# A hand-written order of 1116 tasks, written out anew: a gated long convolution and two MLPs on one Trainium2 core

## The chip, the core and the metric

The kernel runs on one core of one Trainium2 chip. Its work is done by five engines, each with an instruction queue of its own: TensorE (PE, matmuls and transposes through the array; its weight loads are listed as PEld), VectorE (DVE), ScalarE (ACT), GpSimd (POOL) and SyncE (SP), which here only issues transfers. The metric is the time of one execution on the device in microseconds. Of the kernel before there are three runs: 317.10, 317.48 and 317.87 us, median 317.48.

## What is computed

One block of a sequence model with 2048 tokens of width 640 in bfloat16, cut to what matters:

```python
mod = (silu(c) @ w_mod).reshape(c.shape[0], 6, 1, -1)      # sa, ca, ga, sb, cb, gb
h = layernorm(x) * (1 + ca) + sa
x = x + ga * A(h, k, v)                                    # gated long convolution
h = layernorm(x) * (1 + cb) + sb
x = x + gb * B(h)                                          # two MLPs

# A: k_shift = 4-tap causal filter of k;  kv = k_shift * v
#    y = irfft(rfft(kv, 4096) * rfft(ssm_k, 4096))[:2048] + kv * ssm_D;  return q * y
# B: h = gelu(layernorm(x) @ w1);  x1 = x + shifted_by_column_group(h) @ w2
#    return x1 + gelu(layernorm(x1) @ w3) @ w4             # w3: 640 x 1728, w4: 1728 x 640
```

The filter ssm_k has one row of 2048 taps for each of the 640 channels; ssm_D is added to tap 0 of each row, so that the transform of the filter carries that term too.

## The kernel before, in words

**Stages.** The transforms are made as matmuls in two steps of 64 x 64, with tables of sines and cosines that the kernel computes itself. Channels are cut into five blocks of 128 (b = 0 to 4).

- *Tables.* GpSimd writes integer ramps (iota), VectorE masks them to a period (L321, L322), ScalarE takes the sine (L353). For one half of the largest table, Gs, the angles come from ScalarE by an Identity with a scale and an offset (L324, offset offc from L269); the other half comes from three steps on GpSimd or VectorE (L338, L340, L342). L382 makes a negated copy, and three transfers (L389 twice, L390 once) copy parts of the table to other partitions. F1 is a small table (F1c, spread out by L364 and L365); the tables E are scaled by eight small instructions at L406; silu(c) is a chain of seven on GpSimd (L416 to L422).
- *Filter.* Five transfers bring ssm_k (L229, tile Ra), one brings ssm_D (L227). ssm_D is turned into columns by a small matmul (L293) and copied out by ScalarE (L296, Dcol); the same is done with c and the 4-tap filter (L302, L304; copied at L306, csk). L481 adds Dcol to column 0 of a block, and L430 transposes the block in 32 x 32 squares on VectorE into Rb.
- *Stage 1* multiplies the transposed blocks with F1 (L443), 20 PSUM groups for the filter and 20 for kv; *stage 2* multiplies with Gs (L463), 22 groups for each. Every group is copied out of PSUM by ScalarE (L211) or VectorE (L213).
- *kv.* k and v come in eight token pairs each (transfers L495, transposes on TensorE L503, copies L510 or L512). The 4-tap filter is a matmul with diagonal weights (L524), and VectorE multiplies it with v (L529).
- *Modulation.* Twelve half products of silu(c) with w_mod (transfer L549, matmul L555, copies L566 or L570).
- *Inverse.* The two spectra are multiplied on VectorE (L678) after a swap of halves by transfers (L674); the first inverse step is L689 and L690, the second (inverse2) L722 in six pieces.
- *MLPs.* For each token tile: gate and residual (L798, L801), layernorm sums (L790, a square with accumulation on ScalarE), norm (L653 or L655), transposes (called turns: L829, copied by L835 on ScalarE or L837 on VectorE), w1 (L875 and L885, gelu L877 and L891), w2 (L930, residual on VectorE L937), norm and turns again, w3 (L967, L971, gelu L980), w4 (L997, L1006, then VectorE L1029, L1034, L1035 and four output transfers a tile on SP, L1038). The last tile has a path of its own (L1043 to L1056).

**What sets the order.** The function builds a list of 1116 tasks by calls of `add`; a task's number is its place in that list. A string ORDER then names all tasks once, each as a word `<number><engine>`, the engine as P, A, D, G or S, and behind a colon the PSUM slot or slots (0 to 3) for the tiles that the task opens:

```python
for word in ORDER.split():
    head, _, places = word.partition(":")
    t = self.tasks[int(head[:-1])]
    t.on = self.CODE[head[-1]]
```

The tasks are issued in that order, and each engine runs its own in the order of the words; waits between engines follow from what the tasks read and write. So ORDER decides three things: where a task stands in its engine's queue, which engine does a task that may run on several, and which of the four PSUM slots a group uses. PSUM has one pool with one buffer for each slot, so a group in slot 2 waits until the group that had slot 2 before has been copied out. Costs that `add` is given are not used by this.

**Names.** Tasks 0 and 1 to 5 are the loads of ssm_D and of the five blocks of ssm_k, 6 and 7 those of the 4-tap filter and of c; 9 is the iota for the partition index, 10 the small steps on VectorE that make the offsets (L262 to L270), 12 and 13 the selects that make identities (L282, L286). Task 14 (L294) is a sine of one column that nobody reads; it makes ScalarE load the sine table. 15 and 16 are L293 and L296; 17 and 18 are L302 to L304 and L306. 19 to 24 are the table F1 and 25 to 32 the first half of Gs, with 33, 34 and 35 its three transfers; 36 to 48 are the second half, with 46, 47 and 48 its transfers. 66 to 75 are, for each block, L481 and L430. 229 to 232 are loads of x. 446 to 463 are the last six modulation products, three tasks each. 480, 511, 515, 518, 521 and 524 are the pieces of inverse2. 548, 569 and 589 are turns (L829) of the first three tiles; 553, 574 and 594 are their matmuls with w1 (L875, gelu 554, 575 and 595), 555, 576 and 596 the ones beside them (L885, gelu 556, 577 and 597).

Of the kernel before, what the change touches and what calls it, by code (L numbers as in the profile page):

```python
# [26 lines left out]
2S 8D 9G 25G 10D 0S 12G 36G 4S 26A 19G 13G 20D 6S 11G 7S 21D 23A 28A 3S 27D 5S 29D 15P:0 16A 1S 30A 68D 37G 69D 116S 22A 31A 72G 17P:0 24G 32A 18A 73D  # L27
90P:0 34G 50G 70G 86P:1 56G 91A 74G 57G 71D 122S 87A 104P:2 102P:0 66G 105A 38G 88P:1 75D 119S 103A 92P:2 89A 39G 106P:0 67D 93A 125S 117P:1 49G 128S
107A 112P:2 123P:3 113A 118D 82P:0 137S 124D 40A 114P:1 131S 76P:2 83A 115D 41G 120P:3 77A 78P:0 42G 134S 121D 98P:1 33S 79A 100P:2 99D 126P:3 101A
96P:0 58G 150S 127D 129P:1 97A 230S 84P:2 130D 110P:3 85A 80P:0 65G 43D 138P:1 44A 140P:2 139D 111A 59D 45A 51D 132P:3 81A 46S 52D 135P:1 47S 133A  # L30
142P:0 35S 136D 153S 60A 141D 159S 54A 94P:1 53A 61G 108P:3 55D 146P:2 62G 109A 143D 95A 221P:3 147D 48S 63G 199P:1 222A 162S 201P:0 156S 203P:2 200A
202D 209P:3 232S 64A 229S 185P:1 210D 204A 144P:0 186D 205P:2 145D 223P:1 206A 225P:3 224A 219P:2 226D 151P:0 220A 189P:1 152D 165S 154P:3 190A 215P:2
155D 168S 191P:0 216A 207P:1 148P:3 208D 192A 227P:1 149D 197P:0 228A 157P:2 198A 213P:1 158D 171S 187P:3 214A 231S 195P:0 188D 160P:2 244S 196A
211P:1 161D 193P:3 212A 163P:0 194D 217P:2 164A 169P:1 218D 366S 367G 166P:3 170A 172P:0 167D 174P:2 247S 173A 236D 250S 239A 176P:0 175D 235A 184D
182P:2 234A 177D 286P:3 178P:1 287A 183D 238A 278D 288P:3 284P:2 180P:0 289A 179D 285A 294P:3 181D 290P:1 295A 292P:2 291A 281D 245P:3 296P:0 293A
248P:1 246A 279D 282P:2 256S 297A 251P:3 253S 283A 316P:0 259S 252D 249A 314P:2 280D 317A 298P:1 300P:3 315A 320P:0 301A 321D 308P:2 309A 318P:3 299D
306P:0 382S 383G 257P:2 307A 233D 275S 273G 319A 342P:0 258D 271G 276S 332P:1 343D 237G 324P:2 270S 333A 326P:3 325D 274S 340P:0 327A 277S 328P:1 341D
272S 338P:2 329A 254P:3 465D 339A 310P:0 255D 267S 264G 322P:1 265G 311A 266S 312P:3 323D 262G 260P:2 269S 263G 313A 268S 334P:0 240G 261D 302P:1 374S
474D 335A 304P:3 471D 330P:2 303D 305A 336P:0 337A 331D 375G 344P:1 360P:3 390S 391G 345A 362P:0 369D 356P:2 363A 346P:1 368D 398S 399G 357A 354P:0
361A 376D 364P:2 347A 372P:3 365D 449S 355A 475D 358P:1 377D 370P:2 373A 348P:0 385D 371A 406S 407G 378P:3 349A 384D 380P:2 414S 415G 359A 352P:0 392D  # L40
353A 388P:1 472D 379A 393D 386P:0 381A 350P:3 401D 422S 423G 351A 394P:2 400D 430S 431G 389A 396P:3 466D 395A 404P:1 408D 387A 402P:2 409D 397A 450P:0
417D 438S 403A 439G 412P:3 446S 241A 451D 410P:2 452S 416D 14A 411A 425D 418P:0 413A 420P:2 424D 405A 432D 458S 428P:3 419A 455S 426P:1 433D 421A 441D
427A 436P:0 464G 429A 434P:2 476D 440D 437A 447P:1 468D 444P:3 435A 448D 242D 442P:1 445A 473D 453P:2 243G 443A 469D 456P:3 477D 470D 480P:10 478D
457A 467D 454A 479D 518P:23 481A 482D 520A 514G 537D 524P:01 558D 519A 538D 483G 559D 539A 489S 484S 540D 459P:2 560A 578D 541G 498S 561D 550A 579D
461S 460A 493S 562G 542D 525A 511P:23 488S 581D 580A 543D 485S 512A 486S 563D 582G 544A 491S 515P:20 545D 513A 564D 546G 526A 583D 494S 565A 566D 497S
609D 567G 606D 517A 584D 492S 516A 547D 487S 586D 548P:0 585A 490G 610D 462P:2 549A 607D 611A 587G 555P:0 551D 612D 608A 568D 463A 588D 569P:1 613G
556A 589P:2 570D 590D 521P:13 571D 618D 552D 553P:2 530S 619D 614A 529S 620D 594P:0 554A 528S 615D 621A 533S 616D 576P:2 527S 595A 572D 617A 531S
596P:0 622D 496S 597A 669D 623G 523D 535S 534S 577A 574P:0 573D 536S 672D 624A 627D 670D 628P:2 495S 575A 625P:3 673D 629A 598P:0 671A 626D 675G 674A
532S 638P:3 599D 636P:2 639A 676G 601D 500D 600A 677D 681D 637A 602G 682D 683D 522A 643P:2 603D 684A 678D 604P:1 679D 640P:3 605A 644D 680A 685G
656P:1 641D 645A 686G 646D 642A 658P:3 690D 657A 647G 687D 660P:2 659A 499D 691P:1 661A 688P:0 692A 654P:3 501G 651D 689A 648D 591A 652P:1 701P:0 653D  # L50
502A 649P:2 592D 699P:1 593D 650D 505D 702A 717P:2 630D 506D 633A 655A 631D 507G 700A 632D 723P:3 742D 508A 743D 706P:1 739D 740D 718A 703P:0 745D
741A 707D 662P:2 744A 704D 708A 746G 709D 724A 634D 705A 635D 503A 751D 710G 752D 721P:3 663D 711A 504G 753D 747A 714D 766D 712P:2 754A 715P:0 713D
719P:1 722A 748D 749D 716A 664D 750A 789P:0 509A 755D 666S 693D 665S 756G 694D 668S 809D 667S 720A 793P:3 810D 790A 791P:1 510G 757D 696A 760D 695D
794A 812D 811A 813D 761P:3 758P:0 762A 815D 787P:2 697D 759A 698D 814A 836D 763D 792A 816G 771P:0 764D 879D 769P:3 772A 880D 765D 833D 821A 725P:01
817A 822D 823D 770A 818D 824A 819D 881A 767D 825G 820A 768D 726P 727D 788A 826G 882D 837D 728D 830A 883D 730S 731S 776P:2 884A 885G 733D 732S 729S
827A 943D 886G 838D 831P:1 773P:0 777D 832A 944D 891A 828P:2 774D 795P:13 1007D 775A 779G 829D 734D 778A 887A 892D 736S 780G 893D 738S 735S 894A
839P:2 797D 784A 798D 781A 888D 801S 841P:1 889D 802S 796P 842A 800S 834D 895G 799S 835D 737S 946D 840A 947D 890A 948A 785P:2 896G 803D 782P:1 846P:0
783A 786D 949D 897A 900D 843P:1 804D 945A 847D 808S 950G 859P:2 807S 844D 805S 557G 955D 806S 956D 901P:1 849D 860A 861P:0 902D 848A 845A 898P:2 951A
863P:1 850G 899D 952D 905P:2 953D 903P:3 906A 1008D 854D 1010G 957D 864A 857P:2 862A 959G 904A 910P:3 858A 855P:2 911D 907P:0 856A 851D 1009A 852P:2
# [5 lines left out]
1002D 1103D 1004S 1005S 1076P:0 942S 999S 1072P:3 1077A 1003S 1045A 1000S 1006S 941S 998S 1046P:1 1070P:0 1047A 1040P:1 1071A 1073A 1094P:0 1041A  # L65
1074P:3 1048P:12 1075A 1049P 1050D 1051D 1054S 1052S 1053S 1098P:1 1095A 1056D 1096P:3 1099A 1057D 1092P:1 1097A 1061S 1058S 1078P:32 1093A 1060S
1059S 1055S 1079P 1080D 1081D 1083S 1085S 1084S 1082S 1100P:31 1086D 1087D 1101P 1090S 1104D 1088S 1105D 1091S 1106S 1089S 1110D 1109S 1111D 1107S
1115A 1112S 1113A 1114S 1108S
"""


# [1073 lines left out]
```

## Time and profile before

One execution was recorded by the profiler. Its own time was 318.15 us, of which 316.5 us is the span from the first to the last recorded instruction.

| | before |
|---|---|
| runs, us | 317.10, 317.48, 317.87; median 317.48 |
| profiled execution, us | 318.15 (span 316.5) |
| TensorE busy | 285.9 us, 90% of the span |
| VectorE busy | 228.4 us, 72% |
| ScalarE busy | 233.9 us, 74% |
| GpSimd busy | 103.8 us, 33% |
| granted clock of TensorE | full, but half from 117.68 to 134.75 us |
| moved | 32.20 MB, of which q1 (issued by SP) 28.40 MB |

How to read it: a busy share is a mean over stages that have different limits, so the busy time is read stage by stage. A row of instructions names the line of the code, the engine, the operation, and what is written and read; in brackets stand the idle time of the engine just before it and the instruction that ended it.[...] Two facts of the profile that the rows of a page do not say: the five blocks of ssm_k landed at 4.21, 6.56, 7.83, 9.13 and 10.39 us, and task 14 ran at 100.49 us.

### The profile page before, as it was taken

The numbers are of one execution on the slowest core, as the hardware profiler recorded it, in microseconds if no ns is written. First come the engines' busy times: TensorE is split into PE (matmuls) and PEld (weight loads), VectorE is DVE, ScalarE is ACT, GpSimd is POOL, SyncE is SP. The second block draws the span as 40 slices with busy tenths as digits, with TensorE's granted clock in tenths as the row PEclk, the third lists the DMA queues.
The fourth block names the chain that finished last, engine by engine and source line by source line (L and its number), as shares of the span: only waits on it lengthen the run. The fifth ranks groups of instructions, "written<-read, shape, count | busy, mean of one in ns | idle before, by whom it ended". The sixth has DMA issues, their size and how long they took to land.

```text
span 316.5 us, 8551 instructions
## 1 busy us (share of the span) xinstructions
PE 285.9 (90%) x3497; PEld 223.7 (71%) x3503; DVE 228.4 (72%) x453; ACT 233.9 (74%) x382; POOL 103.8 (33%) x235
## 2 busy tenths in 40 slices
PE   0899899989898965978999999999999999999993
PEld 0586676567788843856978867788698776888762
DVE  4998979999999999969898989875541604600433
ACT  6898679999999989799999988958755570234100
POOL 5997100008420558224347735342311210000000
PEclk9999999999999995599999999999999999999999
DMA  7788949056899549495000001100010000010111
GB/s 255 227 245 215 207 119 252 24 155 164 212 232 225 167 137 265 146 305 153 2 3 14 11 2 31 33 21 2 15 29 2 0 3 15 23 47 2 28 37 43
DMA packets 25205, 32.20 MB, mean 102 GB/s; under 512 B 2761, under 2 KB 21838, under 8 KB 25166
## 3 DMA queue, kind: packets, MB, share of 16 engines
q1 hardware_dynamic: 24030, 28.40, 32.8%
q0 software_dynamic: 1040, 3.21, 4.2%
q8 instruction: 27, 0.44, 0.6%
q14 instruction: 12, 0.10, 0.1%
q10 hardware_dynamic: 96, 0.04, 0.1%
HBM read 21.55 MB, written 2.62 MB: 76 GB/s over the span
## 4 chain that ended last, share of the span: by engine, by line
PE 58%; DVE 9%; ACT 4%; issue 2%; DVEq 0%; ACTq 0%
PE ps_w L1006 18%; PE ps_w L971 18%; PE ps_w L930 7%; PE ps_w L875 5%; PE ps_tr L829 3%; DVE Rb L678 3%; PE ps_i L689 1%; DVE Ra L801 1%; PE ps_i L690 1%; PE ps_w L997 1%; ACT RG L790 1%; PE ps_w L967 1%; PE ps_w1x L885 1%; ACT R L891 1%; PE ps_i L722 1%
## 5 line engine op out<-in xcount | busy, mean ns | idle before, releaser
L971 PE MATMUL ps_w<-R,T 128*128 128x256 bf16 (+1 forms) x585 | 61.1, 261 | 0.0
L1006 PE MATMUL ps_w<-T,R 128*128 128x320 bf16 x416 | 59.0, 299 | 0.0
L971 PEld LDWEIGHTS <-T 128*128 128x128 bf16 x585 | 51.3, 98 | 5.9
L1006 PEld LDWEIGHTS <-R 128*128 128x128 bf16 x416 | 40.0, 98 | 16.5 <-issue 1.6
L1029 DVE TENSOR_TENSOR T<-ps_w,R 128x640 bf16<-128x640 f32 x15 | 12.4, 824 | 37.1 <-PE ps_w L997 29.9
L980 ACT ACTIVATE R<-ps_w 128x1024 bf16<-128x1024 f32 (+2 forms) x29 | 25.5, 887 | 17.6 <-PE ps_w L971 10.8
L211 ACT CAST T<-ps_s 128x1024 bf16<-128x1024 f32 x35 | 33.5, 1047 | 2.2 <-PE ps_s L443 2.2
L211 ACT CAST R<-ps_s 128x960 bf16<-128x960 f32 (+1 forms) x30 | 26.9, 961 | 4.8 <-PE ps_s L463 4.5
L790 ACT ACTIVATE RG<-R 128x640 bf16<-128x640 bf16 x32 | 23.6, 737 | 5.5 <-DVE R L937 4.7
L443 PE MATMUL ps_s<-F1bd,Rb 128*128 128x256 bf16 x160 | 23.6, 298 | 3.7 <-ACT csk L306 2.5
L930 PE MATMUL ps_w<-RG,R 128*128 128x320 bf16 x160 | 23.6, 299 | 1.6 <-ACT R L877 1.5
L835 ACT COPY R<-ps_tr 128x640 bf16<-128x640 bf16 x15 | 10.2, 691 | 18.6 <-PE ps_tr L829 18.6
L463 PE MATMUL ps_s<-T,RG 64*128 64x160 bf16 x512 | 21.8, 230 | 2.2 <-DVE R L529 1.0
L776 POOL TENSOR_TENSOR lnv<-lnv,mhalf 128x2 f32<-128x2 f32 (+1 forms) x29 | 22.6, 780 | 2.3
L443 PEld LDWEIGHTS <-Rb 128*128 128x128 bf16 x160 | 16.4, 106 | 9.3 <-DVE Rb L430 3.5
L463 PEld LDWEIGHTS <-RG 64*128 64x128 bf16 x512 | 17.7, 94 | 6.2 <-issue 4.9
L875 PE MATMUL ps_w<-R,RG 128*128 128x256 bf16 (+1 forms) x200 | 20.8, 267 | 1.3 <-ACT R L891 1.3
L937 DVE SCALAR_TENSOR_TENSOR R<-ps_w,R 128x640 bf16<-128x640 f32 x16 | 13.0, 821 | 12.2 <-PE ps_w L930 12.1
L689 PE MATMUL ps_i<-EA,Rb 128*128 128x128 bf16 x160 | 19.2, 219 | 1.7 <-DVE Rb L678 0.8
L930 PEld LDWEIGHTS <-R 128*128 128x128 bf16 x160 | 15.2, 98 | 7.5 <-ACT R L877 2.0
L875 PEld LDWEIGHTS <-RG 128*128 128x128 bf16 x200 | 17.9, 106 | 3.2 <-issue 1.6
L690 PE MATMUL ps_i<-EB,Rb 128*128 128x128 bf16 x160 | 19.1, 219 | 0.3 <-DVE Rb L678 0.3
(196 smaller groups left out, 591.6 us busy)
## 6 DMA issues: line engine op xcount, KB each, us to landing
Ra<-in_A_ssm_k_dram SPq DMA_DIRECT2D x5, 512.0 KB, 5.1
R<-in_w_mod_dram SPq DMA_DIRECT2D x6, 400.0 KB, 5.5
out_dram<-RH SPq DMA_DIRECT2D x60, 40.0 KB, 1.6
T<-in_B_w_dram SPq DMA_DIRECT2D x5, 432.0 KB, 5.2
Ra<-in_A_k_dram SPq DMA_DIRECT2D x6, 320.0 KB, 5.5
Ra<-in_A_v_dram SPq DMA_DIRECT2D x6, 320.0 KB, 4.0
RH<-in_w_mod_dram SPq DMA_DIRECT2D x4, 400.0 KB, 4.0
Ra<-in_A_q_dram SPq DMA_DIRECT2D x4, 320.0 KB, 5.2
```

Source lines behind the costliest of these rows:

```text
L211: nc.scalar.copy(dst, src(ps.tile))
L443: nc.tensor.matmul(psv[:, ml, :], lhsT=xL[:, s0:s0 + P], rhs=F1r, start=True, stop=True)
L463: nc.tensor.matmul(psv[:, g, j], lhsT=Gs[p, k, 64 - 64 * cc:192 - 64 * cc], rhs=T1h[h][p, cc * 32 + k], start=(cc == 0), stop=(cc == 1), t ...
L689: nc.tensor.matmul(psv[:, w, :], lhsT=Av[:, r_, :, g_], rhs=EAf, start=True, stop=False)
L690: nc.tensor.matmul(psv[:, w, :], lhsT=Bv[:, r_, :, g_], rhs=EBf, start=False, stop=True)
L776: nc.gpsimd.tensor_tensor(rs, rs, mhalf[:, 0:n], ALU.pow)
L790: add("ACT", 0.74, lambda e: nc.scalar.activation(junk, src, ACT.Square, scale=float(D) ** -0.5, accum_out=stat[:, li, 1, t:t + 1]), r=[sk ...
L875: nc.tensor.matmul(pt[:, fb, 0:cw], lhsT=w1_sb[:, b, 160 * fb:160 * fb + P], rhs=hT[:, b, 0:cw], start=(b == 0), stop=(b == ND - 1))
L930: nc.tensor.matmul(pt[:, hf, 0:320], lhsT=gsf[:, fb, c0:c0 + P], rhs=w2_sb[:, fb, 320 * hf:320 * hf + 320], start=(fb == 0), stop=(fb == 4))
L971: nc.tensor.matmul(pt[:, fl, 0:cw], lhsT=w3_sb[:, b, fb * P:(fb + 1) * P], rhs=xT[:, b, 0:cw], start=(b == 0), stop=(b == ND - 1))
L980: nc.scalar.activation(g3[g % 2][:, f0:f0 + fn, 0:cw], ps.tile[:, 0:fn, 0:cw], ACT.Gelu_apprx_tanh)
L1006: nc.tensor.matmul(bank(i, hf), lhsT=gg[:, fb, i * P:(i + 1) * P], rhs=w4_sb[:, fb, 320 * hf:320 * hf + 320], start=(fb == 0 and i == 0), ...
```

## The change

Only the string ORDER differs; every task and every instruction in it stays as it was. What the new string does:

- *The first words.* The load of ssm_D (0) is issued ahead of the first block of ssm_k (2). The small sine (14), which stood at 100 us among ScalarE's tasks, is now ScalarE's first. The transfer 34 goes to SP and 46 to GpSimd.
- *Engines.* 75 of the 1116 tasks change engine: 30 from ScalarE to VectorE, 25 from VectorE to ScalarE, 8 from GpSimd to VectorE, 4 from VectorE to GpSimd, 4 from GpSimd to SP and 4 from SP to GpSimd. ScalarE has 271 tasks where it had 276, VectorE 329 where it had 320, GpSimd 90 where it had 94; TensorE (271) and SP (155) keep their number.
- *Function tables.* As built, the kernel before loads a table on ScalarE three times (ahead of L324, ahead of the first sine L353, ahead of the first gelu L891); the kernel after twice (ahead of task 14, and ahead of the first gelu, L877).
- *PSUM.* 187 of the 263 places of PSUM groups are others.
- *The order.* Nearly all of the string is written anew. The sequences of the stages stay the same; within a stage, blocks, groups and tiles change places.

The diff covers all 44 lines of the string. Its first words, the place where task 14 was, TensorE's words around the passage from the inverse to the MLP, and the end:

```diff
 ORDER = """
-2S 8D 9G 25G 10D 0S 12G 36G 4S 26A 19G 13G 20D 6S 11G 7S 21D 23A 28A 3S 27D 5S 29D 15P:0 16A 1S 30A 68D 37G 69D 116S 22A 31A 72G 17P:0 24G 32A 18A 73D
-90P:0 34G 50G 70G 86P:1 56G 91A 74G 57G 71D 122S 87A 104P:2 102P:0 66G 105A 38G 88P:1 75D 119S 103A 92P:2 89A 39G 106P:0 67D 93A 125S 117P:1 49G 128S
...
-417D 438S 403A 439G 412P:3 446S 241A 451D 410P:2 452S 416D 14A 411A 425D 418P:0 413A 420P:2 424D 405A 432D 458S 428P:3 419A 455S 426P:1 433D 421A 441D
...
-556A 589P:2 570D 590D 521P:13 571D 618D 552D 553P:2 530S 619D 614A 529S 620D 594P:0 554A 528S 615D 621A 533S 616D 576P:2 527S 595A 572D 617A 531S
...
+0S 8D 9G 19G 10D 25G 14A 2S 12G 50G 4S 36G 21D 28A 3S 11G 20D 26A 6S 15P:0 16A 29D 7S 23A 22A 27D 1S 31A 5S 68D 30A 69D 116S 32A 37G 34S 24G 72D 73D
+38G 88P:0 90P:1 89A 17P:2 70D 122S 71D 13G 106P:3 91A 33S 84P:0 18A 107A 74G 56G 86P:2 57G 66D 85A 75D 119S 96P:3 49G 87A 98P:0 102P:1 67D 128S 99A
...
+526A 583D 488S 462P:1 517A 551D 498S 567G 584D 496S 516A 547D 607D 585A 548P:0 490G 586D 549A 610D 608A 587G 553P:0 568D 611A 612D 463D 569P:2 554A
+588D 613G 570D 589P:1 552D 521P:23 571D 590D 618A 555P:0 614D 535S 596P:1 556A 619D 532S 615D 530S 620D 597A 594P:0 492S 616D 531S 621A 576P:1 572D
...
 """
```

TensorE's own words in that passage, in order: before `480 518 524 459 511 515 548 462 555 569 589 521 553 594 576 596 574`, after `480 518 511 459 524 515 462 548 553 569 589 521 555 596 594 576 574`.

## The prediction

> **What bounds the kernel now.** I read busy time by stage first, since the shares of the whole span mix stages with different limits; then the start in order of time; then the chain that ended last, where the stages change.
>
> Busy time by stage (each engine's busy us in the stretch; PEclk is the granted clock):
>
> ```profile
> core 0: us, PE busy (x) PEld busy (x) DVE busy (x) ACT busy (x) POOL busy (x), PEclk, DMA share, GB/s
> 0.00:9.30 9.30, 0.48 (x6) 0.41 (x7) 5.18 (x24) 6.71 (x11) 5.42 (x20) 1.00 0.79 278
> ...
> 24.00:54.00 30.00, 28.69 (x417) 20.17 (x420) 26.05 (x37) 24.70 (x32) 7.81 (x8) 1.00 0.76 190
> 54.00:86.00 32.00, 29.30 (x359) 21.14 (x359) 31.03 (x33) 31.33 (x45) 9.90 (x26) 1.00 0.55 144
> 86.00:112.00 26.00, 24.43 (x462) 21.45 (x463) 25.79 (x35) 25.34 (x33) 7.71 (x12) 1.00 0.80 200
> 120.00:131.00 11.00, 7.33 (x217) 5.15 (x216) 10.33 (x30) 10.20 (x23) 7.51 (x11) 0.50 0.79 192
> 131.00:150.00 19.00, 15.30 (x167) 13.05 (x161) 15.59 (x42) 16.34 (x37) 5.03 (x16) 0.90 0.80 232
> 150.00:311.60 161.60, 161.51 (x1517) 127.62 (x1514) 91.72 (x225) 98.26 (x180) 42.50 (x110) 1.00 0.06 16
> ```
>
> Four regimes. To 9.3 us TensorE does nothing: tables and the first transposes are made. To about 112 us VectorE and ScalarE are full (25.79 and 25.34 of 26.00 at the end). From 112 to 150 us the work passes from the convolution to the MLP: TensorE is at half clock for a while, and chains through ScalarE decide. From 150 to 311.6 us TensorE has no idle time (161.51 of 161.60). So time won early comes out at the end one for one if the MLP's matmuls begin earlier; in the last stage nothing can be won by order, only lost.
>
> The start, in order of time:
>
> ```profile
> 1.96 1.28 ACT L324 ACT_TABLE_LOAD   x1 [1.96 <-DVE offc L269]
> ...
> 4.09 1.28 ACT L353 ACT_TABLE_LOAD   x1
> ...
> 4.22 0.18 PE L293 MATMUL ps_row<-T 5*128 5x5 bf16 x1 [4.22 <-DMA T<-in_A_ssm_D_dram]
> ...
> 6.32 0.14 ACT L296 CAST Dcol<-ps_row 128x5 bf16<-128x5 f32 x1
> 6.44 0.43 DVE L322 TENSOR_SCALAR R<-R 128x512 int32<-128x512 int32 x1 [1.91 <-ACT Dcol L296]
> ...
> 6.97 9.79 DVE L430 STREAM_TRANSPOSE Rb<-Ra 128x1024 int32<-128x1024 int32 x5
> ...
> 9.33 6.11 PE L443 MATMUL ps_s<-F1bd,Rb 128*128 128x256 bf16 x28 [2.52 <-ACT csk L306]
> ```
>
> ScalarE loads two function tables. The first waits until 1.96 us for VectorE, as the load stands behind the wait of the Identity that needs it; the second stands ahead of the first sine. The five transposes, and TensorE behind them, wait for ScalarE's queue: the copy L296 runs at 6.32, though its matmul was done at 4.40.
>
> The chain that ended last, around the passage:
>
> ```profile
> 129.50 1.61 PE ps_i L722 x76
> 131.10 4.11 PE ps_w L875 x40
> ...
> 135.73 0.82 ACT RG L790 x2
> ...
> 138.70 0.93 ACT RK L653
> ...
> 144.82 1.03 ACT R L877
> 145.90 1.53 PE ps_w L930 x10
> ```
>
> TensorE's last inverse piece and two blocks of w1 at half clock, then ScalarE's queue until TensorE takes over at 146.
>
> **The start, worked out.** In the changed kernel's built order ScalarE's list begins with a table load with no wait ahead of it, then the small sine (task 14), then both Identities of L324; no second load follows before the gelu's. The other engines issue their first instruction at 0.8 to 0.9 us, so: load 0.8 to 2.1, small sine 0.18 (it ran 100.49 to 100.67) to 2.3, two Identities of 0.80 to 3.9. The matmul L293 began 2.96 us after the issue of the ssm_D transfer; issued first, at 0.79 in place of 1.26, it begins at about 3.75 and ends at 3.95. L296 ends at 4.1 in place of 6.45. The first ssm_k block is issued at 1.26 in place of 0.79; in the trace it was down 3.42 us after issue, so 4.7. The first transpose then starts at 4.9 (0.16 for the add of L481), not 6.97: 2.1 earlier. Three L481 adds of 0.16 go from GpSimd to VectorE between the transposes, so the five end at 15.2 in place of 16.76: **1.6 us earlier**. The other blocks were down at 6.56, 7.83, 9.13 and 10.39, ahead of their turns at about 7.1, 9.3, 11.5 and 13.5. ScalarE after 4.1: 0.6 for F1c, 0.72 and 0.71 for the sines, 0.63 for L382: free at 6.7, not 9.11. GpSimd's F1bd stands behind L338 (0.76) and ends near 6.3, hidden behind the first transpose (ends 6.95). TensorE starts at 7.0, not 9.33. I carry on VectorE's 1.6, the least of the three.
>
> Here the Trainium skill ("ScalarE: Activation LUTs", What ACT_TABLE_LOAD costs) gives a switch of tables 1.28 us for the load and about 1.38 for a drain, 2.66 together. The row has the 1.28, and L353 starts 0.01 after it: no drain. By the rule the dropped load is worth 1.4 us more on ScalarE; I take the row. VectorE's first transpose would wait for the block at 4.7 anyway.
>
> Queues that steps are moved past: the copy of RG (task 34, L389) goes from GpSimd to SP, where it waits for L382 (6.7) ahead of the next k load; that load waits for the second transpose (9.2), so it is hidden; L382 later than 9 us would delay the loads one for one. Task 46 goes from SP to GpSimd, behind the silu chain (L416 to L422, 23.04 to 27.41 now); its input is ready at 25.89 now. I take 0; bounds 0 to 1.5, as the chain's end is the latest it can be held to.
>
> **To 112 us.** Summing the engine changes before the first inverse2 from their rows. VectorE: three stage-1 copies come and three go (1.22 each), six stage-2 copies come and seven go (1.15): -1.15; two token copies come (0.83): +1.66; two table steps come from GpSimd, which have no row on VectorE: the nearest, L342 there, is 0.68, L322 is 0.43; with 0.7 +1.4, bounds 0.9 to 1.5; eight scalings L406 leave, 2.27. Sum **-0.4** (the three adds are in the 1.6 already). ScalarE: +7 x 0.98 - 6 x 0.97 - 2 x 1.24 = -1.4, besides the load. The scalings on GpSimd (rows from 0.2 for one column to 0.76 for 512, so 2 to 6 us) end before their reader L689 at 85 us, as GpSimd has 22 of 30 us free to 54. VectorE decides: -1.6 - 0.4 = -2.0, of which I leave 0.5, since it idles 4 us between 24 and 54, where a load or TensorE comes last and a shorter VectorE wins nothing: **-1.5**. Bounds: -2.3 (TensorE's start, if that idle time takes up the rest) to 0 (if a load or a PSUM buffer is late there).
>
> **112 to 150 us.** One mod product (L555, 1.54) now stands ahead of the first turn (L829), in a gap of 2.42 us. The first w1 block (L875) comes ahead of two turns and the last inverse2: with 2.31 at half clock it runs 126.7 to 129.0 in old time, so the turns begin 0.8 later, the inverse ends at 131.7, L885 twice at 132.9, the second w1 block at 134.9 (135.19 now). On ScalarE the 0.92 norm moves in and another out, 0.41 leaves; the square sum L790 stands ahead of the second gelu, but behind both L891 groups (4 x 0.28): these end at 134.7, the two sums at 136.4, gelu 137.0, the third L891 group 138.1. The norm L653 starts at 138.1 in place of 138.7. I take **-0.5**; bounds -1.8 (the square sum would be free to run at 134) to +1.0 (VectorE carries 0.9 us more, L570 and a norm, ahead of the turns' copies).
>
> The Trainium skill speaks of this place too ("TensorE: Matmul & The Clock Gate", Part 1): half rate until some 3.4 us of sustained work. Dense work starts at 128.2, which would give full clock at 131.6; the profile grants it only at 134.75, 6.5 us on. By the rule, the block moved ahead would bring full clock inside the stretch and 2 us; by the row the stretch stays at half clock, as summed.
>
> **150 us to the end.** The same matmuls; 0, bounds 0 to +3.5 (third rival). The tail, ten issues on SP after the last but one tile and 4.9 us after TensorE's end, has the same count: 0.
>
> Sum: -1.5 - 0.5 = -2.0. The profiled execution took 318.15 us (span 316.5, 1.65 around it) and would take 316.15. It was 0.67 above the median of the runs, 317.48; against that: 315.48, so **315.5 us**.
>
> **Rivals.** First, as worked out: 315.5, own range 314.1 to 316.7; chance 0.54. Second, more is won: the drain exists, or the clock rises early, so 1.4 to 2 us on top, 1.8 for both: 313.7; chance 0.07. For it speaks that ScalarE ends 2.4 us earlier; against it, VectorE is as full as ScalarE. Third, the other side, **distance on TensorE after 150 us**. Its order is written anew and any wait there counts whole. ScalarE runs behind: busy 19.61 of 20 us from 150 to 170, and w1's gelu (L877) started 158.98 though its matmuls ended 157.05, 1.93 late. In the new order one w3 block of 2.18 us stands between that w1 and the w2 that reads it: 1.93 + 1.02 - 2.18 = 0.8 us of wait. At about 213 us a turn's copy goes to ScalarE (0.69) with 0.94 us of matmuls up to its reader: 1.7; near 198 another pair has 1.36 against 1.93 + 0.49: 1.1. Together 0.8 + 1.7 + 1.1, about 3.5: 319.0. It decides from 2.6 us lost (2.0 + 0.6). Against it: ScalarE has 4.4 us less ahead of that w2 where TensorE has 2.6 less, so the lag there should fall to about 0.1. Chance 0.25. Fourth, the gain ends at 24 to 54 us: TensorE and the k and v loads bind there by turns, and what starts early waits for a load: 317.5; chance 0.14. That the load isn't dropped is excluded by the built order.
>
> **How the numbers follow.** 0.2% of 317.5 is 0.6 us, about what a measurement of this kernel can tell from no change. Faster: 0.54 and 0.07, less 0.02 for the first's upper edge: 0.59. Same: 0.14 and 0.02: 0.16. Slower: 0.25. The range goes from the second rival's time to the third's, 313.7 to 319.0; the first's bounds at both ends lie within.
>
> **What would show it.** Right: one table load before 100 us, starting before 1 us; first transpose at 4.9, its five ended by 15.3; first L443 near 7.0; first inverse2 at about 109.7 (111.15 now); L653 at 136.7; TensorE idle of under 0.3 us after 149. Wrong: an L293 that waits past 5 us or transposes that wait for blocks fell the first sum; an inverse2 at 111 or later the second; gaps on TensorE beyond 150 us released by ScalarE are the third rival.

## The result, and the profile after

The changed kernel took 315.27 us (median of 8 runs, 314.13 to 316.53), the kernel before in the same comparison 317.52 us (8 runs, 316.06 to 318.28): a ratio of 0.9932, 95% interval 0.9906 to 0.9958. The prediction said 315.5. Its profiled execution took 316.53 us with a span of 314.8; it is the slowest of its 8 runs, which matters below. A ratio is that of the comparison of runs and not the quotient of two medians; the two can differ by 0.2%. The granted clock is TensorE's clock as the profile records it, full or half.

Busy time by stage of the changed kernel (the columns are those of the table in the prediction; the last stretch ends 1.6 us earlier, as the work does):

```profile
core 0: us, PE busy (x) PEld busy (x) DVE busy (x) ACT busy (x) POOL busy (x), PEclk, DMA share, GB/s
0.00:9.30 9.30, 2.54 (x16) 1.54 (x17) 7.56 (x27) 6.62 (x12) 7.16 (x21) 1.00 0.75 246
...
24.00:54.00 30.00, 29.93 (x422) 20.34 (x421) 25.79 (x30) 23.96 (x34) 8.07 (x12) 1.00 0.71 185
...
131.00:150.00 19.00, 15.12 (x166) 12.14 (x166) 15.13 (x44) 16.98 (x41) 6.98 (x19) 0.91 0.67 241
150.00:310.00 160.00, 159.90 (x1486) 125.91 (x1482) 89.17 (x221) 95.44 (x178) 40.50 (x109) 1.00 0.06 17
```

TensorE starts within the first stretch now (2.54 us of work in place of 0.48), and in the last stage it is idle for 0.1 of 160 us: no wait has come in there. The start, in order of time:

```profile
0.79 1.28 ACT L294 ACT_TABLE_LOAD   x1 [0.79 <-PEq L1129]
...
2.18 0.18 PE L293 MATMUL ps_row<-T 5*128 5x5 bf16 x1 [2.18 <-DMA T<-in_A_ssm_D_dram]
2.27 1.52 ACT L324 ACTIVATE R<-R,offc,s 128x512 int32<-128x512 int32 x2
...
3.69 0.14 ACT L296 CAST Dcol<-ps_row 128x5 bf16<-128x5 f32 x1
...
4.61 0.16 DVE L481 TENSOR_TENSOR Ra<-Ra,Dcol 128x1 bf16<-128x1 bf16 x1 [0.37 <-DMA Ra<-in_A_ssm_k_dram]
4.81 2.07 DVE L430 STREAM_TRANSPOSE Rb<-Ra 128x1024 int32<-128x1024 int32 x1
...
6.93 1.89 PE L443 MATMUL ps_s<-F1bd,Rb 128*128 128x256 bf16 x8 [4.57 <-DVE Ra L481]
```

One load, at 0.79 us and with no wait ahead of it. L296 is 2.6 us earlier, but the first transpose only 2.16, because the block of ssm_k is now what comes last (the bracket of L481). The passage, on TensorE alone (the times in brackets are its idle time and what ended it):

```profile
131.30 1.28 PE L875 MATMUL ps_w<-R,RG 128*128 128x128 bf16 x20 [0.92 <-ACT R L891]
132.44 0.44 PE L885 MATMUL ps_w1x<-R,RG 128*128 128x128 bf16 x5
134.77 1.28 PE L875 MATMUL ps_w<-R,RG 128*128 128x128 bf16 x20 [1.90 <-ACT R L877]
136.38 1.25 PE L829 MATMUL ps_tr<-RG,RK 128*128 128x128 bf16 x10 [0.34 <-DVE RK L655]
137.47 2.66 PE L930 MATMUL ps_w<-RG,R 128*128 128x320 bf16 x10
```

The block of w2 at 137.47 took 2.66 us; in the kernel before the same ten matmuls took 1.53:

```profile
140.29 1.53 PE L930 MATMUL ps_w<-RG,R 128*128 128x320 bf16 x10 [0.17 <-ACT R L877]
```

The record of the granted clock says why: in this execution it was at half from 112.50 to 129.56 and once more from 136.39 to 139.81 us, in the profiled execution of before once, from 117.69 to 134.75.

Where the time went, as the shift of a task against before in the two profiled executions: first transpose -2.16, end of the five transposes -1.27, first kv group copied (57 us) -2.04, first inverse2 **-2.71**, first norm by L653 in the passage -2.82, the block of w2 at 147.5 **-1.69**, end of TensorE's work -1.66. So 2.7 us were won to the first inverse2, and 1.0 given back between 138 and 146 us.

### The profile page after: what moved, and what is told of

Same layout as the page of the kernel before. It is cut to its first block, busy times and chain, and to the rows that moved or that the text cites. A ratio compares the mean times of both kernels' runs of the same rounds, so it can differ in the third digit from the quotient of the medians.

```text
span 314.8 us, 8560 instructions
## 1 busy us (share of the span) xinstructions
PE 286.4 (91%) x3503; PEld 222.4 (71%) x3503; DVE 226.7 (72%) x451; ACT 229.7 (73%) x382; POOL 102.0 (32%) x242
## 3 DMA queue, kind: packets, MB, share of 16 engines
HBM read 21.55 MB, written 2.62 MB: 77 GB/s over the span
## 4 chain that ended last, share of the span: by engine, by line
PE 70%; ACT 13%; DMA 7%; DVE 6%; issue 1%; POOL 0%; SPq 0%; DVEq 0%; ACTq 0%
PE ps_w L1006 18%; PE ps_w L971 18%; PE ps_w L930 7%; ACT T L211 6%; PE ps_w L875 5%; DMA RG<-in_B_w_dram 4%; PE ps_s L463 3%; ACT R L211 3%; PE ps_tr L829 3%; PE ps_ksh L524 3%; PE ps_tk L503 3%; PE ps_s L443 2%; DMA Ra<-in_A_k_dram 2%; PE ps_w1x L885 1%; DVE Rb L430 1%
## 5 line engine op out<-in xcount | busy, mean ns | idle before, releaser
L211 ACT CAST R<-ps_s 128x960 bf16<-128x960 f32 (+1 forms) x31 | 27.9, 974 | 4.6 <-PE ps_s L463 4.4
L443 PE MATMUL ps_s<-F1bd,Rb 128*128 128x256 bf16 x160 | 22.2, 284 | 5.9 <-DVE Ra L481 4.7
L930 PE MATMUL ps_w<-RG,R 128*128 128x320 bf16 x160 | 24.7, 308 | 1.3 <-ACT R L877 1.3
L443 PEld LDWEIGHTS <-Rb 128*128 128x128 bf16 x160 | 15.6, 101 | 11.0 <-DVE Ra L481 5.1
L776 POOL TENSOR_TENSOR lnv<-lnv,mhalf 128x2 f32<-128x2 f32 (+1 forms) x29 | 21.8, 752 | 2.3
L775 POOL TENSOR_TENSOR lnv<-stat,lnv 128x2 f32<-128x2 f32 x19 | 5.7, 300 | 45.4 <-ACT RG L790 41.9
```

The source lines that it names most:

```text
L211: nc.scalar.copy(dst, src(ps.tile))
L443: nc.tensor.matmul(psv[:, ml, :], lhsT=xL[:, s0:s0 + P], rhs=F1r, start=True, stop=True)
L776: nc.gpsimd.tensor_tensor(rs, rs, mhalf[:, 0:n], ALU.pow)
L930: nc.tensor.matmul(pt[:, hf, 0:320], lhsT=gsf[:, fb, c0:c0 + P], rhs=w2_sb[:, fb, 320 * hf:320 * hf + 320], start=(fb == 0), stop=(fb == 4))
```

## The experiments

Two questions were open. What makes the 2.7 us up to the first inverse2, of which the prediction had only 1.5? And is the 1.0 us behind it a cost of the new order (theory 1) or of the clock in that one execution (theory 2)? All ratios are to the kernel before, run beside each kernel on the same chip.

| kernel | first transpose, us | first L443, us | first inverse2, us | median, us | ratio, 95% interval |
|---|---|---|---|---|---|
| before (profiled) | 6.97 | 9.33 | 111.15 | 317.5 | 1 |
| after (profiled) | 4.81 | 6.93 | 108.44 | 315.27 | 0.9932, 0.9906 to 0.9958 |
| front_sine_alone | 4.87 | 7.12 | 108.95 | 315.60 | 0.9942, 0.9924 to 0.9961 |
| front_identity | 6.02 | 8.38 | 110.22 | 316.62 | 0.9976, 0.9959 to 0.9994 |
| ssm_D_first_alone | 6.97 | 9.33 | 112.08 | 317.67 | 1.0000, 0.9985 to 1.0015 |
| front_three_words | 4.87 | 6.98 | 109.37 | 315.00 | 0.9913, 0.9895 to 0.9931 |
| after_sine_late | 5.84 | 8.00 | 109.82 | 316.39 | 0.9963, 0.9941 to 0.9985 |
| before_then_after | 6.97 | 9.33 | 111.16 | 317.36 | 1.0002, 0.9985 to 1.0020 |
| after_then_before | 4.70 | 6.82 | 108.77 | 314.90 | 0.9909, 0.9886 to 0.9931 |
| start_then_before | 4.94 | 7.06 | 112.00 | 318.83 | 1.0063, 1.0040 to 1.0086 |
| front_sine_then_after | 4.79 | 7.74 | 109.57 | 316.03 | 0.9979, 0.9961 to 0.9998 |
| after_then_before_fill | 4.69 | 6.82 | 109.39 | 320.56 | 1.0121, 1.0093 to 1.0150 |
| after_then_before_again | 4.89 | 7.01 | 108.52 | 314.71 | 0.9898, 0.9883 to 0.9914 |
| after_again | 4.87 | 6.98 | 108.26 | 315.62 | 0.9926, 0.9912 to 0.9940 |

### One word moved

```diff
-... 25G 10D 0S 12G 36G 4S 26A ... 452S 416D 14A 411A ...
+... 25G 10D 14A 0S 12G 36G 4S 26A ... 452S 416D 411A ...
```

> The kernel before with one word moved: task 14, the small sine, from 100 us to the head of ScalarE's list. Everything else stays in the order of before. The theory of the prediction (the start is worth about what the first transposes win, and VectorE and ScalarE carry it to 112 us): one table load at 0.8 us and none until the gelu, L296 at about 4.4 in place of 6.32, the first transpose at about 5.1 in place of 6.97, the first inverse2 1.5 to 2.0 us earlier than 111.15, and 1.3 to 2.0 us off the whole (ratio 0.994 to 0.996). Rival (what starts early waits for the k and v loads between 24 and 54 us, and the gain of the changed kernel comes from the new order of the convolution): the first transpose just as early, but the first inverse2 at 110.8 to 111.2 and the whole within 0.5 us of before.

The first view is its start, in order of time:

```profile
0.79 1.28 ACT L294 ACT_TABLE_LOAD   x1 [0.79 <-PEq L1129]
...
4.24 0.18 PE L293 MATMUL ps_row<-T 5*128 5x5 bf16 x1 [4.24 <-DMA T<-in_A_ssm_D_dram]
4.46 0.17 ACT L296 CAST Dcol<-ps_row 128x5 bf16<-128x5 f32 x1 [0.50 <-PE ps_row L293]
...
8.16 7.44 ACT L211 CAST T<-ps_s 128x1024 bf16<-128x1024 f32 x8 [1.36 <-PE ps_s L443]
```

This one word gives a ratio of 0.9942, where the whole change gave 0.9932. ScalarE is ready before L293 is (it waits 0.50 us). And the shift goes through: -2.10 at the first transpose, -2.21 at the first L443, -2.20 at 57 and at 108 us, -2.19 at the first inverse2. Nothing between 24 and 54 us took any of it. The loads of k and v are issued into memory that the transposes set free, so they are released by the work that had come earlier, and move with it: the third load L495 is issued at 8.91 us in place of 10.96.

Where the shift is settled can be read as well. The kernel before has the same block of eight copies out of stage 1, which leave ScalarE no idle time:

```profile
10.38 7.43 ACT L211 CAST T<-ps_s 128x1024 bf16<-128x1024 f32 x8 [1.19 <-PE ps_s L443]
```

In the four traces with the old convolution and an earlier start, what these copies won at the third of them is what the first inverse2 won, within 0.02 us: 2.18 and 2.19 here, 0.95 and 0.93 in front_identity, 1.59 and 1.58 in front_sine_then_after, 1.76 and 1.78 in front_three_words. The end of the five transposes does not tell it: 2.04, 0.84, 1.94 and 1.92.

### Early or dropped

The same word, but the instruction is an Identity whose result nobody reads, so the sine table is still loaded ahead of the first sine.

```diff
-... nc.scalar.activation(lnv[:, 2, 0:1], b_pos[:], ACT.Sin) ...
+... nc.scalar.activation(lnv[:, 2, 0:1], b_pos[:], ACT.Identity) ...
```

> The kernel before with task 14 at the head of ScalarE's list, as in front_sine_alone, but with an Identity in place of the sine (its result is read by nobody). So the first load comes at 0.8 us without a wait, and the load of the sine table stays where it was, ahead of the first sine. It parts the 2.1 us of front_sine_alone into the load that comes earlier and the load that is dropped. Theory (a load costs its row, 1.28 us, and nothing else): Identity L324 at 2.3, the second load from 3.1 to 4.4, L296 at about 5.4 to 5.6, the first transpose at 5.9 to 6.1 (1.0 earlier than 6.97), the first inverse2 1.0 to 1.2 earlier than 111.15 and the whole 0.7 to 1.2 us faster than before. Rival (a switch of tables costs 2.66 us with its drain): the second load would be followed or led by 1.4 us of idle time on ScalarE, and the first transpose comes no earlier than 6.9, the whole within 0.5 us of before.

ScalarE's start:

```profile
2.20 0.80 ACT L324 ACTIVATE R<-R,offc,s 128x512 int32<-128x512 int32 x1
3.01 1.28 ACT L353 ACT_TABLE_LOAD   x1
4.31 0.32 ACT L353 ACTIVATE F1c<-R,b_neg 128x32 bf16<-128x32 int32 x1
```

The load begins 0.01 us after the Identity and the sine 0.02 after the load: no drain. The first transpose comes 0.95 us earlier; with the load dropped as well, 2.10. So the earlier load is worth 0.95 and the dropped one 1.15, and both shifts arrive at the first inverse2 (-0.93, -2.19). The 2.66 us that the Trainium skill gives for a switch ("ScalarE: Activation LUTs", What ACT_TABLE_LOAD costs) is not what this kernel pays.

### ssm_D first, alone

```diff
-2S 8D 9G 25G 10D 0S 12G ...
+0S 2S 8D 9G 25G 10D 12G ...
```

> The kernel before with one word moved: the load of ssm_D (task 0) ahead of the first block of ssm_k (task 2). The prediction's claim that L296 waits for ScalarE's queue and not for the matmul L293: L293 earlier by 0.5 to 2 us, but L296 still at 6.2 to 6.4, the first transpose at 6.9 to 7.1, the first inverse2 at 111.0 to 111.4 and the whole within 0.6 us of before. Rival (ssm_D first is a part of the gain): L296 and the first transpose more than 0.5 us earlier, and 0.5 us or more off the whole.

L296 at 6.32 and the first transpose at 6.97, both to 0.01 us as before; up to 97 us none of VectorE's tasks moved by more than 0.14 us. (At 98.8 us VectorE then waited 0.83 us for a transfer of the inverse, L674, in this execution: the 0.93 us at its first inverse2 are no effect of the word. So one trace's first inverse2 can be off by as much.) The claim holds: the copy waited for ScalarE's queue, and this part of the change is worth nothing by itself.

### Small waits at the start

```diff
-... 31A 72G 17P:0 24G 32A 18A 73D 90P:0 34G 50G 70G 86P:1 56G 91A 74G ...
+... 31A 72D 24G 32A 73D 90P:0 34G 50G 70G 86P:1 17P:2 56G 91A 18A 74G ...
```

and task 14 to the front.

> front_sine_alone with two more words changed: the add L481 of block 3 (task 72) goes from GpSimd to VectorE, so that F1bd (task 24) no longer stands behind a block of ssm_k in GpSimd's queue, and the five small matmuls for c and the 4-tap filter (17) with their copy (18) go behind the first two groups of stage 1 and to PSUM slot 2, so that the first L443 no longer waits for the small load of c. Theory (in the order of before, small waits at the start decide by the luck of the loads' landings whether the convolution starts at 7.1 or 7.7, and what starts earlier is carried to the first inverse2): first L443 at 6.9 to 7.1, first inverse2 at 108.6 to 109.0, the whole 2.0 to 2.7 us faster than before (314.8 to 315.4), as fast as the changed kernel with three words of it. Rival (the changed kernel's order of the convolution and its passage are needed): not more than 1.9 us faster than before, and slower than the changed kernel of the same call.

0.9913, so these four words (14, 72, 17 and 18; its name counts 17 and its copy 18 as one) bring as much as the whole new string. But the path is not the one expected: the first L443 came at 6.98, 0.14 earlier than in front_sine_alone, and the first inverse2 at 109.37, 0.42 later. ScalarE's and TensorE's rows:

```profile
9.14 0.18 ACT L306 CAST csk<-ps_row 128x25 bf16<-128x25 f32 x1
...
9.38 2.71 PE L443 MATMUL ps_s<-F1bd,Rb 128*128 128x256 bf16 x16 [0.27 <-ACT csk L306]
...
10.43 5.59 ACT L211 CAST T<-ps_s 128x1024 bf16<-128x1024 f32 x6 [0.19 <-PE ps_s L443]
```

The moved copy of csk (18) now stands inside the block of eight copies, and TensorE waits for it: ScalarE's first copy came 2.33 us earlier than before, its third 1.76, and 1.78 is what arrived. So the loss lies in where 17 and 18 went, and what passed that place was carried in full. The move of 72 was not tried alone. The median has more of its gain behind the first inverse2 (-3.10 at the block of w2 in its trace).

### The changed kernel without the word

```diff
-... 19G 10D 25G 14A 2S 12G ... 412P:3 416D 411A ...
+... 19G 10D 25G 2S 12G ... 412P:3 416D 14A 411A ...
```

> The changed kernel with task 14 put back to its old place behind task 416, so that the sine table is loaded ahead of the first sine that is needed, behind the Identities of L324. By the theory of the prediction: two loads again at the start, the first transpose at about 5.5 to 6 and the first L443 at about 9 in place of 6.93, ScalarE 2.6 us later after the tables; the first inverse2 at 109.5 to 110.5 in place of 108.44, and the whole 1 to 2 us above the changed kernel (ratio to before 0.996 to 1.000). By the rival (loads decide between 24 and 54 us): the first inverse2 stays at 108.4 to 108.9 and the whole within 0.5 us of the changed kernel.

1.1 us above the changed kernel's 315.27; the first transpose at 5.84, the first inverse2 at 109.82. So the word is worth 1.0 to 1.4 us there, less than the 2.19 in the old order: in the new list both Identities and L296 stand ahead of the second load (5.13 us), and L296 runs at 4.97. The rest of the new string is therefore worth 1.1 us without the word.

### The two halves

Before to the first inverse2, then after, and the reverse:

```diff
 ... 456P:3 477D 470D 480P:10
-478D 457A 467D 454A 479D 518P:23 ...
+467D 478D 479D 454A 457A 518P:23 ...
```

> The order of before up to and with the first inverse2 (task 480), then the rest in the order of after. It has only the second half of the change: the passage to the MLP and the MLP. The profiled execution of the changed kernel gave back 1.0 us between the first inverse2 (2.7 earlier) and 150 us (1.7 earlier). Theory 1 (the new order of the passage costs that, and the prediction's 0.5 of gain there was wrong): first inverse2 at 111.1, the whole 0.7 to 1.2 us slower than before (ratio 1.002 to 1.004). Theory 2 (it was this one execution's granted clock, which fell to half once more from 136.7 to 139.6 us, and the order itself is worth 0 to 0.5 us of gain): the whole 0 to 0.6 us faster than before (ratio 0.998 to 1.000). Distance on TensorE after 150 us, the third rival of the prediction, would make it 2 us or more slower.

```diff
 ... 456P:2 479D 454A 480P:10
-469D 457A 476D 470D 518P:23 ...
+476D 469D 470D 457A 518P:23 ...
```

> The order of after up to and with the first inverse2 (task 480), then the rest in the order of before. It has only the first half of the change: the start and the convolution. Both theories: first inverse2 at 108.4 to 108.6. Theory 1 (the new order of the passage costs 1.0 us): the whole 2.5 to 2.9 us faster than before, faster than the changed kernel by 0.5 us or more (ratio 0.991 to 0.992). Theory 2 (the passage's order is worth 0 to 0.5 us of gain): the whole 1.7 to 2.3 us faster than before, not faster than the changed kernel (ratio 0.993 to 0.995). A third way, that what is won ahead of 111 us runs into the loads of w1 and x and is lost there with the old order: within 1 us of before.

The second half alone changes nothing that can be told (1.0002); the first half alone gives 0.9909, no less than the whole. The two theories share the points: by theory 1 the second half alone should have been slower by 0.7 us or more, and it was not; but the first half alone won 2.62 us, which is theory 1's size (2.5 to 2.9) and over theory 2's (1.7 to 2.3). The pair was run again side by side:

> after_then_before once more, beside the changed kernel on the same chip, to tell whether the passage of before is the better one behind the convolution of after. If the passage of after costs nothing (theory 2): within 0.6 us of after_again, and 1.8 to 2.6 us faster than before. If it costs (theory 1): 0.6 us or more faster than after_again. The mean granted clock should be 0.971 mostly (five stretches of 3.41 us at half), with single runs at 0.976 that are over 1 us faster.

> The changed kernel once more, as the partner of after_then_before_again and front_three_words. 1.9 to 2.6 us faster than before. If the grid of the granted clock makes the profiled execution's passage look worse than the runs (theory 2), most runs have a mean granted clock of 0.976 or 0.977 and those at 0.966 to 0.969 are 0.5 us or more slower; and in a trace at 0.976 or above, all of the 2.4 to 2.9 us won at the first inverse2 is still there at 150 us. If the order of the passage costs 1.0 us (theory 1), it is lost between 108 and 150 us in such a trace too.

Here the old passage is the better one behind the new convolution: 314.71 against 315.62, 0.9898 (0.9883 to 0.9914) against 0.9926 (0.9912 to 0.9940). That is theory 1's forecast, 0.6 us or more. Theory 2's forecast for the clock in after_again was missed: one of its six runs has a mean clock of 0.976 or more, not most, and its runs at 0.966 and 0.968 are slower than the other four by 0.25 us on average, not 0.5. With front_sine_alone ahead of it, the new passage is worse too (the diff is to front_sine_alone):

```diff
 ... 456P:3 477D 470D 480P:10
-478D 457A 467D 454A 479D 518P:23 ...
+467D 478D 479D 454A 457A 518P:23 ...
```

> The order of front_sine_alone up to and with the first inverse2, then the rest in the order of after. Up to there it is before with one word moved (the first inverse2 at 108.95 in that run); the passage and the MLP are those of the changed kernel. If the parts add up: -1.92 for the word and -0.16 for the second half, so 2.1 us faster than before, 315.4. Theory 1 (the new passage costs 1.0 us): 0.9 us faster only. If the granted clock has five stretches of 3.41 us at half in one passage and four in the other, the mean granted clock shows it (0.971 against 0.977), and runs with another number differ by 0.4 us or more for each.

316.03 against 315.60, and by ratio 0.9979 against 0.9942; the gain of 1.4 us lies between theory 1's 0.9 and the 2.1 of parts that add up. Its trace shows something else besides: with the same order up to the first inverse2 as front_sine_alone, it was 0.62 us later there. GpSimd's and TensorE's rows:

```profile
6.64 0.19 POOL L481 TENSOR_TENSOR Ra<-Ra,Dcol 128x1 bf16<-128x1 bf16 x1 [0.78 <-DMA Ra<-in_A_ssm_k_dram]
...
7.27 0.41 POOL L365 TENSOR_SCALAR_AFFINE_SELECT F1bd<-F1bd 128x256 bf16<-128x256 bf16 x1
...
7.74 1.65 PE L443 MATMUL ps_s<-F1bd,Rb 128*128 128x256 bf16 x7 [0.47 <-POOL F1bd L365]
```

An add of GpSimd waits for its block of ssm_k, and the table F1bd stands behind it in the queue. So in the old order the landing of one block moved everything by 0.6 us between these two traces; the new order has three of the five adds on VectorE.

### What the second half does to the clock

In all traces the granted clock changes on one grid: every stretch that ends inside the trace is a multiple of 3.41 us (17.07, 13.65, 10.24, 6.83, 3.41), and the grid begins at another point of the program in each execution (the first change to full clock came between 10.1 and 15.3 us). The loss between the first norm of the passage and the block of w2 at 147.5 is there when, and only when, a second stretch at half falls there; the table has eight of the 13 traces without added work, and the other five agree:

| trace | half clock from, us (lengths) | shift at the norm | shift at the w2 block |
|---|---|---|---|
| after | 112.50 (17.07), 136.39 (3.41) | -2.82 | -1.69 |
| after_again | 118.11 (10.24), 135.17 (3.41) | -3.78 | -2.78 |
| start_then_before | 116.64 (13.65), 137.12 (3.41) | -0.36 | +0.16 |
| after_sine_late | 115.55 (13.65) | -2.38 | -2.38 |
| before_then_after | 115.62 (3.41), 122.45 (10.24) | -0.50 | -0.50 |
| front_sine_then_after | 115.02 (13.65) | -2.75 | -2.75 |
| front_sine_alone | 114.41 (17.07) | -2.72 | -2.72 |
| after_then_before | 114.30 (17.07) | -2.72 | -2.72 |

So in the profiled execution the 1.0 us came by way of the clock, as theory 2 had it. TensorE waits in the new passage twice for ScalarE (1.90 us for the gelu L877, 0.92 for L891), so a stretch of the grid is busy for little there (0.38 in after's, from 132.98 us), the clock falls again and the next block takes 2.66 us in place of 1.53. A low share alone doesn't decide it: with 0.44 in the same place the clock fell in after_again and held in after_sine_late and front_sine_then_after. Nor is the new order needed for it: start_then_before has the old passage, and fell as well.

The medians say something else. The old passage has one long stretch nearly always: 58 of the 63 runs of before whose clock is on record have a mean clock of 0.969 to 0.973 (317.51 us on average), and the five at 0.975 to 0.977 took 316.11. Of the 12 runs of before_then_after, eight have 0.974 or above and took 317.15 on average; the other four, at 0.967 to 0.973, took 318.37. So at a like clock the new passage is about 1.0 us slower behind the same convolution, and comes out level because it more often has the higher clock. In the pair run side by side the mean clock is 0.971 and 0.970, and the new passage is 0.9 us slower. This is rough, since a mean clock does not tell where the half stretches lie, but it speaks for theory 1: the order has a price that the count of half stretches does not explain.

### TensorE kept busy

```diff
+    FILL = {('mid', 14): 12, ('end', 3): 12, ('mid', 5): 30, ('end', 5): 30}
...
+                        if a == 0 and j4 == 2 and cg == 0:
+                            filler(pss[0].tile, 160 * n, FILL.get(("mid", tilesA[0]), 0))
...
+            filler(pss[1].tile, 160 * n, FILL.get(("end", tilesA[0]), 0))
```

> after_then_before with matmuls added on TensorE whose results nobody reads: they stand in the gaps of the passage, inside and behind the pieces of inverse2 (12 and 12 of 192 columns, 30 and 30 of 32 columns), and write to parts of PSUM tiles that are not copied out. In the six traces so far the granted clock changes on a grid of 3.41 us: it falls to half after a stretch in which TensorE was busy 0.38 to 0.61 of the time, and rises after one with 0.93 to 1.00. Theory (the clock falls because TensorE waits in the passage, and the fall costs time): the added work lifts the stretches from 110.9 to 121 us above 0.65, the clock falls later or not at all, TensorE's blocks between 123 and 132 take half the time, and the whole is 0.8 to 2.5 us faster than after_then_before (312.4 to 314.1). Rival (chains through ScalarE and VectorE set the passage, the clock costs nothing): the whole within 0.5 us of after_then_before, or slower by what the added work delays.

The mechanism held: with the added work the stretches that end at 114.2 and 117.6 us were busy for 0.68 or more, and the clock fell at 121.03 us in place of 114.30. But the kernel took 320.56 us. ScalarE's copies out of the pieces of inverse2, and TensorE between them:

```profile
120.75 1.29 ACT L211 CAST Rb<-ps_i 128x640 bf16<-128x640 f32 x2 [1.71 <-PE ps_i L714]
...
126.54 0.46 PE L730 MATMUL ps_i<-T,RH 32*32 32x160 bf16 x7 [3.29 <-issue]
...
127.95 1.82 ACT L211 CAST Rb<-ps_i 128x960 bf16<-128x960 f32 x2 [5.19 <-PE ps_i L714]
```

L714 is the added work; L730 is L722 of the other kernels. The copies wait for L714, though they read other columns of the tile, so the chain was made longer by what was to fill its gaps. That is not all: TensorE's idle times without a releaser came to 6.2 us in these pieces (0.83, 2.11 and 3.29) where after_then_before has 3.6, and the second copy's wait holds the longest of them; the last section comes back to them. The two were not parted. What a full clock in the passage would be worth stays untested.

### The start of after in front of before

```diff
 ... 57G 66D 85A 75D
-119S 96P:3 49G 87A 98P:0 ...
+87A 104P:2 102P:0 105A 119S ...
```

> The first words of after, up to and with the last of the three first transposes that it lists (task 75), then the rest in the order of before. So the start of after (ssm_D first, small sine first, its tables' order) with the convolution and the passage of before. In the changed kernel the first transpose comes 2.16 us earlier, but the last of the five 1.2 only. Theory of the prediction (VectorE carries what the end of the five transposes wins): the first inverse2 1.2 to 1.6 us earlier than 111.15. Rival (what carries is TensorE's and ScalarE's start, as in front_sine_alone, where everything moved by 2.19 up to the first inverse2): 2.0 to 2.4 us earlier, the whole 1.7 to 2.6 us faster than before.

Neither: the first transpose at 4.94, but the first inverse2 at 112.00, 0.85 later than before. TensorE's row:

```profile
13.18 1.03 PE L443 MATMUL ps_s<-F1bd,Rb 128*128 128x256 bf16 x8 [1.71 <-ACT T L211]
```

At the seam all copies of stage 1 are ScalarE's, and TensorE waits for PSUM slots: 1.71 us here and 0.67 twice by 17 us. What the start had won was gone by then: the first product of the inverse (L678, at 82 us in before) came 0.57 us later than in before. The experiment doesn't answer its question, since the seam is a cost of its own; it shows that a start is worth only what the groups behind it can take over.

## Why the prediction was right, and where not

The time was right within 0.3 us. Some of its steps were not, and their errors went in opposite directions.

- **The start** was right: a load at 0.79 with no wait (predicted 0.8), first transpose 4.81 (4.9), first L443 6.93 (7.0), end of the five transposes 15.49 (15.2). Its estimate for L293 was too late (3.75; it ran at 2.18, as the transfer of ssm_D was down 1.4 us after its issue and not 2.96), which cost nothing, since the block came last either way.
- **"I carry on VectorE's 1.6, the least of the three"** was right in the engine. In the five traces with the new convolution and no added work (those of after, after_again, both of after_then_before, and after_sine_late) the first product of the inverse, L678 at 82 us in before, came 0.74 to 0.75 us earlier than the end of VectorE's transposes tells, though that end moved by anything from 0.13 to 1.51 us; ScalarE's copies out of stage 1 do not tell it. (In the old convolution it is the other way round, see above.) The size was 1.27: the first transpose came 2.16 earlier, but the three adds more take 0.37 and the fourth transpose waited 0.29 for an add of GpSimd (L481).
- **"Sum -0.4", "of which I leave 0.5, since it idles 4 us between 24 and 54"** and with them the **-1.5** failed. The first inverse2 came 2.71 us earlier (2.89, 2.62 and 2.38 in the three further traces of this order), beyond the bound of 2.3. From the end of the transposes to the last L678 VectorE took 1.44 us less. Its busy time there fell by 1.26 us (from 84.24 to 82.98), where -0.4 was taken (0.4 of the difference are the two table steps, taken as 1.4 and measured as 0.97). Its idle time fell by 0.18 (from 5.63 to 5.45), where 0.5 was left: the waits move with what releases them, as in front_sine_alone, where nothing was left on the way. So 1.27 + 1.26 + 0.18 = 2.71.
- **"I take -0.5"** for 112 to 150 us: +1.0 in the profiled execution, the upper bound. In the runs, 2.25 of median gain less 2.65 (the mean of the four traces) is +0.4. The order on ScalarE went as said (first norm by L653 at 135.88; predicted 136.7), but the step took the half clock as a fixed stretch. It ended at 129.56 us in place of 134.75, 2.5 us more than the work had moved, so the early rise of the second rival came; the norm had won only 0.1 us more than the first inverse2 by then. What the step did not see is that the clock could fall a second time, and that the new order costs something at a like clock too. The rule and the row that it weighed agree on the grid: in before the stretch from 127.93 us was busy for 0.91, the next one wholly, and the clock rose at its end, 6.5 us after dense work began.
- **150 us to the end: 0** was right: 0.1 us of idle time in 160. The third rival (waits on TensorE there, 3.5 us) fell: none of its three places shows a wait. The second rival's drain fell with front_identity and the fourth (the gain ends at the loads) with front_sine_alone.

That the total came out within 0.3 us is luck: two errors cancelled, 1.2 us too little won before 111 us, and 0.9 to 1.5 too much after it.

Open: by which wait the new passage costs time at a like clock. Its medians were 0.4 to 0.9 us above the old passage's behind an early convolution, and 0.16 below behind the old one; the phase of the grid was not held fixed. The lowest ratios are those of after_then_before, the new order up to the first inverse2 and the old one behind it: 0.9898 and 0.9909 in its two comparisons. front_three_words, at 0.9913, can't be told from it.

## What to carry to other kernels

A table load on ScalarE stands behind the wait of the instruction that needs it; a small instruction of the right function with no wait, put first, starts the load at once and can make a second load unnecessary, and here that single word by itself gave 1.92 us where the whole change gave 2.25. Before a gain is written off against loads further on, look at what releases those loads: if it is the work that moves, they move too. Where several engines start earlier by different amounts, the shift that arrives unchanged in several traces tells which of them carries: here ScalarE's copies in the old order, and VectorE's transposes in the new. And a stage that lies at the edge of the clock's grid differs from run to run, so read several traces of it before its order is blamed or praised.

## What the runs showed of the hardware that was not expected

**The clock's grid.** In all 14 traces every change of the granted clock lies on a grid of 3.41 us with a phase of its own in each execution, as the Trainium skill describes it ("TensorE: Matmul & The Clock Gate", What's actually happening: a free-running window of 3413 ns). What these traces add, from TensorE's busy share in each stretch of 3.41 us: at half clock it rose after stretches busy for 0.92 and more (and twice after less, 0.85 and 0.89) and stayed down after others with up to 0.91; at full clock it fell after 0.35 to 0.62 in the passage, far from idle, and held after others with 0.44 to 0.62, so the share alone does not tell. Before its first record (15.29 us in before, 10.10 in after) the page shows a clock of 1.00, but matmuls of L443 start 213 ns apart there and 109 ns apart right behind it: in both kernels TensorE began at half rate. The kernel before had half rate up to 15.29 us too, therefore, and not from 117.69 to 134.75 alone.

**Instruction fetch, as far as the times show it.** TensorE's longest idle times in the pieces of inverse2 have no releaser. Two rows of the changed kernel:

```profile
113.15 0.97 PE L722 MATMUL ps_i<-T,RH 32*32 32x160 bf16 x44 [1.85 <-issue]
...
119.48 1.48 PE L722 MATMUL ps_i<-T,RH 32*32 32x160 bf16 x81 [2.51 <-issue]
```

The transfers of the instruction queue q8 (27 in the run, 0.44 MB, so 16 KB each) ended at 111.63 and 118.05 us there. In the 13 traces without the added work, 26 such gaps, two in each, ended 1.27 to 1.62 us after the end of a fetch. The skill's "Runtime: NRT & Kernel Launch" (Instruction fetch mechanics) has the 16 KiB blocks and calls the fetch mostly hidden; here, where 192 matmuls and as many weight loads are issued in 2.2 us, the times fit a fetch that isn't: 1.9 us of TensorE's time in before and 4.4 in after, 1.9 to 3.7 in the eight traces of the old passage and 2.9 to 4.4 in the five of the new. With the added work of after_then_before_fill there were 28 transfers, and the gap of 3.29 us ended 1.49 us after the end of one. That the fetch is the cause is inferred from these times; whether the gaps set the new passage's price was not tried.
